# The upper right block of the second weight kept whole, with smaller output and score buffers, six attention visits moved, and the last product cut into column pieces

## The chip, the cores and the metric

The kernel runs on one core of a Trainium2 chip. The metric is the device time of one execution in microseconds (us). A core has five engines that run side by side: TensorE (PE in the profile; PEld are its weight loads), VectorE (DVE), ScalarE (ACT), GpSimd (POOL) and the sync engine (SP), beside the DMA engines that move data. Matrix products land in PSUM banks and are brought from there into SBUF by DVE or ACT.

## The reference

```python
scores = scale * np.matmul(q, k.transpose(0, 1, 3, 2))      # 8 batches, 12 heads, 448 x 448
attn = np.maximum(scores, 0.0) ** 2 / S
x = np.matmul(attn, v)                                      # back to [8, 448, 768]
...
xn = (x - mu) / np.sqrt(var + 1e-06) * g_ln                 # per row of 768
ch = np.maximum(xn @ w_ch1, 0.0) @ w_ch2                    # 768 -> 3072 -> 768
return x + ch
```

## The kernel before

**Work and tiles.** The work is done in bf16 with sums in fp32. A batch b has 6 pairs of heads. The pairs are taken in two halves, so that a batch has three attention steps, numbered n = 3b to 3b + 2 over all batches, and each step has seven key blocks s. `att_QK(n, s)` makes one score tile with four 64-row products (L587). One activation on ACT (L596) or DVE (L598) scales it and applies the relu, and takes it from one of three PSUM slots into a score buffer in SBUF. A square in place follows (L611 on DVE, L613 on POOL). `att_AV(n, s)` multiplies the squared tile with v: 28 products for the seven s of a step (L649). A copy (L363 or L365) takes the result out.

**The feed forward part.** `ffn_1` multiplies the normalised batch with w1, 24 column blocks of six products (L930). Each block's relu is written to `h1` by ACT (L946) or DVE (L948), over two PSUM banks in turn, so that a block waits for the relu of the one before the last. The second product, of 24 row chunks of w2, is made in tiles of 128 rows and in two column halves of 384. For batches 0 and 1, and for one tile m = 2 of each later pair of batches, `ffn_2` does it plainly with 24 products a half (L1200), and DVE takes each half out with the row scale and the residual (L1217). For the other tiles of batches 2 to 7 `ffn_w` takes two tiles together by the scheme of seven products for eight: named P1, P2, P6, P5, P7, P3 and P4, with 12 matmuls of 384 columns each (L1122), two PSUM banks named x and y, and evacuations on DVE named c1, C11, c2, p5, C22, C12 and C21 (L1136). It needs differences of the four blocks of w2 (`b11`, `b12` upper left and right, `b21`, `b22` below), named T1 to T4 and made once by `make_sums` (L988, on DVE or POOL), and differences of the rows of `h1` (L1082, the S operations on DVE).

**T1 and the five extra products.** T1 is b12 - b11, in 12 chunks. Seven chunks have a home in a staging buffer. The last five are written over b12 itself. From then on the upper right block of w2 is no longer whole, so the second column half of a plain tile of batches 2 to 7 takes b12 as T1 + b11: five more products of the same rows of `h1` with `b11`, that is 29 matmuls where the first half has 24.

**Buffers.** Score tiles come from a pool of `N_AT` = 9 buffers of 128x896 bf16. Output tiles come from a pool of two of 128x768 fp32, with one of 128x384 (`o_half`) beside it. `store_tile` writes each with two DMAs of 64 rows (L1239), on ACT's queue. The last tile alone has one of its two on SP's.

**Who sets the order.** The instruction order of each engine is written out ahead by a planner in the kernel (`Order`) with a cost for each operation, and each engine then runs its list in order. `segment` mixes the steps of the feed forward part of batch b with the attention of batch b + 1. The attention is cut into visits, and a visit is due when the feed forward work done has reached its share (`due`). The visit that matters here, one for each step n from 7 on except those that begin a batch without a predecessor in progress, is

```python
        if prev:
            return head + [qks(n, 0, 2) + av_of(n - 1) + qks(n, 2, 4), qks(n, 4, 7)]
```

that is on PE: 8 matmuls of L587 for (n, 0) and (n, 1), the 28 of L649 for step n - 1, then 8 of L587 for (n, 2) and (n, 3). With three PSUM slots, (n, 2) waits for the relu of (n, 0), and (n, 3) for the relu of (n, 1). There are 16 such visits with the score buffers of batches 2 to 7: n = 7, 8, 10, 11 and 12 to 23.

Of the kernel before, what the change touches and what calls it, by code (L numbers as in the profile page):

```python
# [199 lines left out]
def kernel(  # L200
# [10 lines left out]
    nc = tc.nc  # L211
# [22 lines left out]
    FIRST_ORDER = "qqaqaqqqqqqaaaqaqaaqaqaqqqaaaqaaqaaqqaaqqaaaaaaaa"  # L234
    N_O = 2
    SUMMED = [0] + [2] + [NPER] * (B - 2)
# [6 lines left out]
    v_pool = ctx.enter_context(tc.tile_pool(name="v", bufs=1))  # L243
    at_pool = ctx.enter_context(tc.tile_pool(name="attn", bufs=N_AT))
    xc_pool = ctx.enter_context(tc.tile_pool(name="xc", bufs=1))
    s_pool = ctx.enter_context(tc.tile_pool(name="small", bufs=4))
    o_half = ctx.enter_context(tc.tile_pool(name="oh", bufs=1))
    o_pool = ctx.enter_context(tc.tile_pool(name="o", bufs=N_O))
    ps_s = ctx.enter_context(tc.tile_pool(name="ps_s", bufs=3, space=bass.MemoryType.PSUM))
# [5 lines left out]
    g_sb = const_pool.tile([P, K1], fp32)  # L255
    g_rows = const_pool.tile([K1, P], fp32)
    ident_f = const_pool.tile([K1, K1], fp32)
    w1 = w_pool.tile([P, K1, d_ff], bf16)
    w2 = w_pool.tile([P, K2, d_model], bf16)
    h1 = w_pool.tile([P, K2, S + T], bf16)  # L260
    sum_t = const_pool.tile([P, S], fp32)
    rsum_t = const_pool.tile([P, S], bf16)
    xT_all = const_pool.tile([P, J * d_model], bf16)
    x_all = const_pool.tile([P, J, d_model], bf16)
# [215 lines left out]
    attn = {}  # L480
    at_ring = [None] * N_AT
    held = []
    held_relu = []

    def wait_for_x(ev):
# [4 lines left out]
        else:  # L490
            held_relu.append(ev)

    def at_use(last):
        at_ring.pop(0)
        at_ring.append(last)

# [72 lines left out]
    def att_QK(n, s):  # L569
# [4 lines left out]
        def emit(eng):  # L574
            if b == 1 and s >= J - 3:
                if (n, s) == (NPER, J - 3):
                    attn["more"] = big(STAGE[0], None, i=6, r=2, c=S)
                attn[n, s] = attn["more"][:, 3 * (pn % 2) + s - (J - 3)]
            else:
                a = at_pool.tile([P, 2, S], bf16, tag="attn")  # L580
                attn[n, s] = a
            sc = ps_s.tile([P, 2, 512], fp32, tag="s")
            st[0] = sc
            for r in range(2):
                qT = qkT[b][rows_of(r), 0].rearrange("p (j t) c -> p j t c", t=NPER)
                for half in range(2):
                    nc.tensor.matmul(  # L587
                        sc[rows_of(half), r, :S],
                        qkT[b][rows_of(r), 1, s * NPER + pn, rows_of(half)],
                        qT[:, :, pn, rows_of(half)], start=True, stop=True)  # L590

        op = R.pe(195.0, emit, qk_dep(n, s) + [slots[0], at_ring[0]], "Q")

# [27 lines left out]
        slot_use(ev)  # L621
        at_use(None)
        if early:
# [332 lines left out]
    o_st = {}  # L956
    o_ring = [DONE] * N_O

# [24 lines left out]
    def make_sums():  # L983
# [49 lines left out]
        for k, o, d in pieces(t4):  # L1033
            for i in range(o.shape[1]):
                made["T4", k + i] = run(o[:, i:i + 1], b21[:, k + i:k + i + 1],
                                        tw["T2", k + i].rearrange("p (o c) -> p o c", o=1), True, [made["T2", k + i]] + d, 5.2)
        for k in range(J):
            tw["T1", k] = stage["cols"][:, 1, k]
        for a, z in ((0, 3), (3, 5), (5, J)):
            made["T1", a] = run(stage["cols"][:, 1, a:z], b12[:, a:z], b11[:, a:z], True,  # L1040
                                w2_ld + [later("turn", 3, 1)], 5.3)
        for k, n in ((J, 3), (J + 3, 2)):
            for i in range(k, k + n):
                tw["T1", i] = b12[:, i]
            made["T1", k] = run(b12[:, k:k + n], b12[:, k:k + n], b11[:, k:k + n], True,
                                done3 + [later("f2_end", 0)], 5.3)
        for name in ("T1", "T2", "T3", "T4"):
# [47 lines left out]
    def ffn_w(u, m, name, part):  # L1095
# [8 lines left out]
        if name == "P1" and part == 0:  # L1104
            if when(f_banks[0]) > when(f_banks[1]):
                f_banks.reverse()
                f_tags.reverse()
            e["y0"] = f_banks[1]
        bank = "x" if name in ("P1", "P6", "P7", "P4") else "y"
        w = {"P1": lambda k: b11[:, k], "P2": lambda k: b21[:, k], "P6": lambda k: tw["T2", k], "P5": lambda k: tw["T1", k],  # L1110
# [16 lines left out]
        def evac(key, tile_n, cols, r, more, deps):  # L1127
            def emit(eng):
                if key == "c1":
                    o_t = o_pool.tile([P, d_model], fp32, tag="o")  # L1130
                    e["o", 0] = o_t
                elif key == "p5":
                    o_t = o_half.tile([P, hd], fp32, tag="oh")
                    e["o", 1] = o_t
                o = e["o", 1] if key in ("p5", "C22") else e["o", 0][:, cols]
                nc.vector.scalar_tensor_tensor(o, e["ps", bank], r, o if more else xm[u, m + tile_n][:, cols],  # L1136
                                               op0=Alu.mult, op1=Alu.add)
            e[key] = R.add("DVE", 620.0, emit, [op, ops["rstd", b]] + deps, key=-3.0)
            return e[key]

        if name == "P1":
            e["S1"] = [s_op(u, m, "S1", x, [op, e["S2"][x]]) for x in range(2)]
            evac("c1", 0, lo, r1, False, [o_ring[-N_O]])
        elif name == "P2":
            e["S4"] = [s_op(u, m, "S4", x, [op, e["S2"][x]]) for x in range(2)]
            ev = evac("C11", 0, lo, r1, True, [e["c1"]])
            e["C11 out"] = store_tile(u, m, lo, ev, False, lambda: e["o", 0][:, lo])
        elif name == "P6":
            evac("c2", 0, hi, r1, False, [e["c1"]])
            s2_last = [op, e["S1"], e["S4"]]  # L1150
# [6 lines left out]
        elif name == "P5":  # L1157
            evac("p5", 1, hi, r2, False, [half_free[0]])
        elif name == "P7":
            ev = evac("C22", 1, hi, r2, True, [e["p5"]])  # L1160
            half_free[0] = store_tile(u, m + 1, hi, ev, False, lambda: e["o", 1])
        elif name == "P3":
            ev = evac("C12", 0, hi, r1, True, [e["c2"], e["C11"]])
            e["C12 out"] = store_tile(u, m, hi, ev, False, lambda: e["o", 0][:, hi])
        else:
            ev = evac("C21", 1, lo, r2, False, [e["C11 out"]])
            f_banks[:] = [e["C12"], ev]
            f_tags.reverse()
            o_ring.append([e["C12 out"], store_tile(u, m + 1, lo, ev, final, lambda: e["o", 0][:, lo])])
            if m == 3:  # L1170
# [4 lines left out]

    def part_of(u, j, part, parts):
        n = K2 if u == 0 or j == 0 else K2 + KH - J
        return slice(part * n // parts, (part + 1) * n // parts)

    def f2_deps(u, m, j, part, parts):  # L1180
        b = 2 * u + (0 if m < 3 else 1)
        z = min(part_of(u, j, part, parts).stop, K2) - 1
        d = [ops["w2", z], ops["h", b, z]]
# [4 lines left out]
    def ffn_2(u, m, j, part, parts):  # L1188

        b = 2 * u + (0 if m < 3 else 1)  # L1190
        ks = [(k, w2[:, k, j * hd:(j + 1) * hd]) for k in range(K2)]
        if u > 0 and j == 1:
            ks = [(k, b11[:, k]) for k in range(J, KH)] + ks

        def emit(eng):
            if part == 0:
                o_ps = f_tile([P, hd], fp32)
                o_st["ps"] = o_ps
            for i, (ki, w) in list(enumerate(ks))[part_of(u, j, part, parts)]:
                nc.tensor.matmul(o_st["ps"], stat(u, m, ki), w, start=(i == 0), stop=(i == len(ks) - 1))  # L1200
        run = part_of(u, j, part, parts)
        op = R.pe(162.5 * (run.stop - run.start), emit, f2_deps(u, m, j, part, parts) + (ops["sums", "T1"] if u > 0 and j == 1 else []))
        if m in (2, 6) and j == 1 and part == parts - 1:
# [6 lines left out]
        ri = m if m < 3 else m - 3  # L1210

        def evac(eng):
            if j == 0:
                o_t = o_pool.tile([P, d_model], fp32, tag="o")
                o_st[u, m] = o_t
            cols = slice(j * hd, (j + 1) * hd)
            nc.vector.scalar_tensor_tensor(o_st[u, m][:, cols], ps, rstd[b][:, ri:ri + 1], xm[u, m][:, cols],  # L1217
                                           op0=Alu.mult, op1=Alu.add)
        ev = R.add("DVE", 620.0, evac, [op, ops["rstd", b], o_ring[-N_O]], key=-3.0)
        f_use(ev)  # L1220
        if j == 1:
            if m in (2, 6):
                now_known(ev, "f2_out", b)
            if m == 3:
                ops["m3_out", u] = ev
            o_ring.append(store_tile(u, m, slice(0, d_model), ev, False, lambda: o_st[u, m]))

    half_free = [DONE]

    def store_tile(u, m, cols, ev, final, src):  # L1230
# [5 lines left out]
        for r, (bb, jj) in enumerate(blocks):  # L1236
            def store(eng, r=r, bb=bb, jj=jj):
                dst = out[2 * u + bb].rearrange("(p j) d -> j p d", j=J)[jj, :, cols]
                (nc.scalar if eng == "ACT" else nc.sync).dma_start(dst, src()[rows_of(r)])  # L1239
            sto = R.add("SP" if final and r else "ACT", 550.0, store, [ev], key=-0.5, load=(T, 150.0))  # L1240
# [69 lines left out]
    def f2_steps(u, ms):  # L1310
        return [("f2", u, m, j, p, n) for m in ms for j in range(2)
                for n in [PARTS if u == 0 or j == 0 else 5] for p in range(n)]

# [3 lines left out]
    def segment(steps, visits, then, margin, ahead=True, hooks=()):  # L1317
# [5 lines left out]
        while i < len(steps) or done < n_v or not centered:  # L1323
# [7 lines left out]
            if done == n_v and not centered:  # L1331
                tC = start_of(mean_deps(then) + [slots[0]])
                if tC <= now + 60.0:
                    center(then)
                    centered = True
                    continue
            due = done < n_v and prog >= (total - margin) * done / n_v
            if min(tF, tV, tC) >= FAR:
# [171 lines left out]
```

## Time and profile before

| | |
|---|---|
| median of 3 runs | 530.66 us (530.31 to 530.81) |
| the profiled execution | 530.49 us, of which the span is 528.6 us |
| PE busy | 513.4 us, 97% of the span |
| DVE, ACT, POOL busy | 341.5, 227.0 and 117.3 us |
| granted TensorE clock | 0.998 of full speed |
| DMA | 51.91 MB read, 11.01 MB written |

The profile is of one execution. Its span goes from the first to the last instruction, and 1.9 us of its time lie around it. "Busy" is the time in which an engine has an instruction under way. Ends of matmuls are modelled, so that neighbouring ones overlap: how long one takes in a stream is read from the starts.

### The profile page before, as it was taken

What the parts mean: (1) busy time and instruction counts of PE and PEld (TensorE: products, weight loads), DVE (VectorE), ACT (ScalarE), POOL (GpSimd) and SP (SyncE); (2) the same over time, 40 slices, a digit from 0 to 9 for tenths busy, and PEclk for the clock granted to TensorE, in tenths of its full rate; (3) what the DMA queues carried; (4) which work ended last, traced back from release to release, by engine and by line L of the source; (5) the groups of instructions that cost most, each with busy time, mean ns of one, the idle gap of its engine ahead of it and who ended that gap; (6) DMA issues with size and microseconds to landing.
All of it is one profiled execution on the core that took longest, in us unless ns stands there. A gap on an engine that the chain in (4) does not pass through costs nothing.

```text
span 528.6 us, 9882 instructions
## 1 busy us (share of the span) xinstructions
PE 513.4 (97%) x4107; PEld 276.9 (52%) x4107; DVE 341.5 (65%) x632; ACT 227.0 (43%) x361; POOL 117.3 (22%) x132
## 2 busy tenths in 40 slices
PE   5899999999999999999999999999999999999996
PEld 3444455555564455545555455644556445555553
DVE  5988647438996667773877666666578646534352
ACT  5978611124314653275323663156531655124300
POOL 7411600401342222230250320403210202100000
PEclk9999999999999999999999999999999999999999
DMA  9999999988198902979079920989024400241022
GB/s 193 197 188 199 199 191 165 171 101 135 34 164 126 105 2 43 157 117 97 16 111 127 122 54 16 164 128 104 4 38 99 82 1 0 61 73 19 1 62 60
DMA packets 144121, 51.83 MB, mean 98 GB/s; under 512 B 121798, under 2 KB 142028, under 8 KB 144076
## 3 DMA queue, kind: packets, MB, share of 16 engines
q0 software_dynamic: 81072, 25.50, 45.4%
q1 hardware_dynamic: 55724, 14.79, 17.6%
q10 hardware_dynamic: 7280, 10.92, 8.4%
q8 instruction: 32, 0.52, 0.4%
q14 instruction: 13, 0.11, 0.1%
HBM read 51.91 MB, written 11.01 MB: 119 GB/s over the span
## 4 chain that ended last, share of the span: by engine, by line
PE 93%; DVE 4%; ACT 1%; DMA 1%; issue 0%; ACTq 0%; DVEq 0%
PE f_ps L930 40%; PE f_ps L1122 23%; PE f_ps L1200 15%; PE sc L587 6%; PE ps L649 5%; DVE a L611 2%; ACT a L596 1%; DVE t L365 1%; DMA f<-in_q_dram 1%; PE ps L508 1%; PE f_ps L910 0%; PE ps L711 0%; DVE st L792 0%; DVE st L791 0%; PE f_ps L508 0%
## 5 line engine op out<-in xcount | busy, mean ns | idle before, releaser
L930 PE MATMUL f_ps<-a,w 128*128 128x448 bf16 x1134 | 220.7, 353 | 0.6 <-DVE h L948 0.6
L930 PEld LDWEIGHTS <-w 128*128 128x128 bf16 x1134 | 108.3, 98 | 108.6 <-issue 11.0
L596 ACT ACTIVATE a<-sc 128x896 bf16<-128x896 f32 x117 | 103.4, 927 | 81.9 <-PE sc L587 75.9
L946 ACT ACTIVATE h<-f_ps 128x448 bf16<-128x448 f32 (+1 forms) x156 | 83.2, 534 | 106.5 <-PE f_ps L930 105.2
L611 DVE TENSOR_TENSOR a<-a 128x896 bf16<-128x896 bf16 x156 | 100.6, 683 | 1.4 <-ACT a L596 1.4
L1122 PEld LDWEIGHTS <-h 128*128 128x128 bf16 x648 | 62.8, 98 | 43.8 <-issue 2.4
L598 DVE TENSOR_SCALAR a<-sc 128x896 bf16<-128x896 f32 x42 | 45.6, 1087 | 41.2 <-PE sc L587 41.1
L1122 PE MATMUL f_ps<-w,h 128*128 128x384 bf16 x369 | 65.2, 326 | 0.0
L1200 PE MATMUL f_ps<-w,h 128*128 128x384 bf16 x351 | 58.7, 326 | 0.0
L587 PE MATMUL sc<-t 64*64 64x448 bf16 x672 | 49.0, 365 | 4.0 <-ACT a L596 2.4
L1200 PEld LDWEIGHTS <-h 128*128 128x128 bf16 x351 | 33.9, 98 | 23.8 <-issue 1.7
L740 POOL TENSOR_TENSOR sum_t<-sum_t,xT_all 128x384 f32<-128x384 f32 (+2 forms) x25 | 20.0, 799 | 94.6 <-ACT xT_all L363 94.6
L1136 DVE SCALAR_TENSOR_TENSOR o_t<-f_ps,r_t,x_all 128x384 f32<-128x384 f32 x36 | 22.1, 614 | 18.6 <-PE f_ps L1122 18.3
L587 PEld LDWEIGHTS <-t 64*64 64x64 bf16 x672 | 17.7, 106 | 28.3 <-issue 21.8
L401 POOL DMA_DIRECT2D t<-in_k_dram x12 | 20.0, 1901 | 52.7 <-DMA t<-t 52.7
L649 PE MATMUL ps<-a,v_t 64*64 64x448 bf16 x552 | 29.8, 350 | 0.0
L1217 DVE SCALAR_TENSOR_TENSOR o_t<-f_ps,r_t,x_all 128x384 f32<-128x384 f32 x20 | 12.3, 613 | 26.4 <-PE f_ps L1200 26.3
L363 ACT CAST xT_all<-ps 128x768 bf16<-128x768 f32 (+2 forms) x34 | 20.7, 614 | 19.9 <-PE ps L649 18.1
L649 PEld LDWEIGHTS <-v_t 64*64 64x64 bf16 x672 | 19.7, 107 | 13.5 <-issue 2.8
L401 POOL DMA_DIRECT2D t<-in_q_dram x12 | 19.3, 1774 | 31.4 <-DMA t<-t 30.1
L1136 DVE SCALAR_TENSOR_TENSOR o_t<-f_ps,r_t,o_t 128x384 f32<-128x384 f32 x27 | 16.6, 614 | 14.8 <-PE f_ps L1122 14.7
L848 ACT ACTIVATE a<-a,g_sb 128x448 bf16<-128x448 bf16 x19 | 11.6, 659 | 30.3 <-DVE a L841 15.1
(91 smaller groups left out, 411.8 us busy)
## 6 DMA issues: line engine op xcount, KB each, us to landing
out_dram<-o_t ACTq DMA_DIRECT2D x71, 96.0 KB, 2.2
v_t<-in_v_dram POOLq DMA_DIRECT2D x16, 336.0 KB, 6.1
w<-in_moe_w_ch_dram POOLq DMA_DIRECT2D x4, 1152.0 KB, 39.0
t<-in_q_dram POOLq DMA_DIRECT2D x12, 336.0 KB, 8.6
t<-in_k_dram POOLq DMA_DIRECT2D x12, 336.0 KB, 6.8
out_dram<-o_t ACTq DMA_DIRECT2D x20, 192.0 KB, 5.5
w<-in_moe_w_ch_dram POOLq DMA_DIRECT2D x4, 768.0 KB, 19.3
w<-in_moe_w_ch_dram POOLq DMA_DIRECT2D x1, 1536.0 KB, 28.9
```

The costliest lines, as they stand in the source:

```text
L363: nc.scalar.copy(o, i)
L401: nc.gpsimd.dma_start(stage["cols"][half * T:(half + 1) * T, t if b < 4 else 0].rearrange("p j (h d) -> p j h d", d=D), src[b, half * 6:ha ...
L587: nc.tensor.matmul(sc[rows_of(half), r, :S], qkT[b][rows_of(r), 1, s * NPER + pn, rows_of(half)], qT[:, :, pn, rows_of(half)], start=True, ...
L596: nc.scalar.activation(attn[n, s], st[0][:, :, :S], Act.Relu, scale=rc2)
L598: nc.vector.tensor_scalar(attn[n, s], st[0][:, :, :S], rc2, 0.0, op0=Alu.mult, op1=Alu.max)
L611: nc.vector.tensor_mul(attn[n, s], attn[n, s], attn[n, s])
L649: nc.tensor.matmul(av_st[n][half][rows_of(hh)], vt[b][rows_of(half), 2 * pn + hh, s * D:(s + 1) * D], attn[n, s][rows_of(half), hh, :], st ...
L930: nc.tensor.matmul(st[0], w1[:, ki, ni * P:(ni + 1) * P], xc[b][:, ki, :], start=(i == 0), stop=(i == K1 - 1))
L946: nc.scalar.activation(o, st[0][:, c], Act.Relu)
L1122: nc.tensor.matmul(e["ps", bank], a(k), w(k), start=new and k == 0, stop=k == KH - 1, skip_group_check=True)
L1136: nc.vector.scalar_tensor_tensor(o, e["ps", bank], r, o if more else xm[u, m + tile_n][:, cols], op0=Alu.mult, op1=Alu.add)
L1200: nc.tensor.matmul(o_st["ps"], stat(u, m, ki), w, start=(i == 0), stop=(i == len(ks) - 1))
```

## The change

- The last five chunks of T1 get a home of their own, at the end of one large buffer (`at_all`) that also holds the score tiles. So b12 stays whole, and `ffn_2` uses 24 products in both column halves, in all batches.
- The score tiles are slices of `at_all` in turn: nine while b < 2, and eight for b >= 2, since the ninth lies where the home of T1's last chunks is.
- Outputs use two tiles of 128x768 (`o_all`) and no half tile: the pair of `ffn_w` writes both, its second tile's right half into the other one, and each half of each tile is waited for by itself (`o_done`). `g_rows` becomes a slice of `sum_t`.
- `HELD` shifts the point at which six visits are due, by -2 to +4 in units of 1000 ns of planned feed forward work. Its keys are (n, 0) for n = 13, 15, 16, 19, 21 and 22.
- The very last P4 is made in two column pieces by `last_product`: 256 columns into bank x as before, then 128 columns into bank y from zero. What bank x holds for those 128 columns is taken out ahead (`early`). Each piece has its own evacuation and two stores, one on ACT's queue and one on SP's.

```diff
+    HELD = {(13, 0): -2, (15, 0): -1, (16, 0): 3, (19, 0): 4, (21, 0): -1, (22, 0): 3}
...
-    at_pool = ctx.enter_context(tc.tile_pool(name="attn", bufs=N_AT))
-    o_half = ctx.enter_context(tc.tile_pool(name="oh", bufs=1))
-    o_pool = ctx.enter_context(tc.tile_pool(name="o", bufs=N_O))
...
+    g_rows = sum_t[:K1, :P]
+    at_all = const_pool.tile([P, (N_AT - 1) * 2 * S + 5 * (d_model // 2)], bf16)
+    o_all = const_pool.tile([P, 2, d_model], fp32)
...
-                a = at_pool.tile([P, 2, S], bf16, tag="attn")
-                attn[n, s] = a
+                i = at_next[0] % (N_AT if b < 2 else N_AT - 1)
+                at_next[0] = i + 1
+                attn[n, s] = at_all[:, i * 2 * S:(i + 1) * 2 * S].rearrange("p (r c) -> p r c", r=2)
...
-        for k, n in ((J, 3), (J + 3, 2)):
-            for i in range(k, k + n):
-                tw["T1", i] = b12[:, i]
-            made["T1", k] = run(b12[:, k:k + n], b12[:, k:k + n], b11[:, k:k + n], True,
-                                done3 + [later("f2_end", 0)], 5.3)
+        at_end = at_all[:, (N_AT - 1) * 2 * S:].rearrange("p (k c) -> p k c", c=hd)
+        for a, z in ((0, 3), (3, 5), (5, J), (J, 10), (10, KH)):
+            o = stage["cols"][:, 1, a:z] if a < J else at_end[:, a - J:z - J]
+            for k in range(a, z):
+                tw["T1", k] = o[:, k - a]
+            made["T1", a] = run(o, b12[:, a:z], b11[:, a:z], True, w2_ld + [later("turn", 3, 1), later("av_done", 1)], 5.3)
...
+            e["turn"] = o_take()
+            e["o", 0], e["o", 1] = o_all[:, e["turn"]], o_all[:, 1 - e["turn"]]
...
+    def last_product(u, m, part, e, r2, deps):
+        c = (slice(0, 2 * P), slice(2 * P, hd))[part]
+        o = e["o", 0][:, c]
+        if part == 0:
+            def early(eng):
+                c1 = slice(2 * P, hd)
+                nc.vector.scalar_tensor_tensor(e["o", 0][:, c1], e["ps", "x"][:, c1], r2, xm[u, m + 1][:, c1],
+                                               op0=Alu.mult, op1=Alu.add)
+            e["early"] = R.add("DVE", 310.0, early, [e["P7 end"], e["C11 out"]], key=-3.0)
+        ps = e["ps", "x"][:, c] if part == 0 else e["ps", "y"][:, :P]
+        def emit(eng):
+            for k in range(KH):
+                nc.tensor.matmul(ps, stat(u, m + 1, KH + k), tw["T4", k][:, c], start=part == 1 and k == 0, stop=k == KH - 1,
+                                 skip_group_check=True)
+        op = R.pe(KH * (110.0, 57.0)[part], emit, deps + ([e["early"]] if part == 0 else [e["C12"]]))
+        def evac(eng):
+            nc.vector.scalar_tensor_tensor(o, ps, r2, xm[u, m + 1][:, c] if part == 0 else o, op0=Alu.mult, op1=Alu.add)
+        ev = R.add("DVE", (470.0, 310.0)[part], evac, [op, e["C11 out"]], key=-3.0)
+        store_tile(u, m + 1, c, ev, True, e["o", 0])
...
-        ks = [(k, w2[:, k, j * hd:(j + 1) * hd]) for k in range(K2)]
-        if u > 0 and j == 1:
-            ks = [(k, b11[:, k]) for k in range(J, KH)] + ks
...
+            for ki in range(part * K2 // parts, (part + 1) * K2 // parts):
+                nc.tensor.matmul(o_st["ps"], stat(u, m, ki), w2[:, ki, j * hd:(j + 1) * hd],
+                                 start=(ki == 0), stop=(ki == K2 - 1))
...
-            due = done < n_v and prog >= (total - margin) * done / n_v
+            due = done < n_v and prog >= (total - margin) * done / n_v + 1000.0 * HELD.get(visits[done][0][1:3], 0)
```

## The prediction

> **What bounds the kernel now.** I read the busy rows first, then the table of busy time by stage, the chain that ended last, and the timeline of the stages that the change touches. From the page and from the chain:
>
> ```profile
> PE 513.4 (97%) x4107; PEld 276.9 (52%) x4107; DVE 341.5 (65%) x632; ACT 227.0 (43%) x361; POOL 117.3 (22%) x132
> PE 93%; DVE 4%; ACT 1%; DMA 1%; issue 0%; ACTq 0%; DVEq 0%
> ...
> L1200 PE MATMUL f_ps<-w,h 128*128 128x384 bf16 x351 | 58.7, 326 | 0.0
> ...
> 96.30 17.55 PE f_ps L1200 x108
> ```
>
> PE is busy 97% of the span and makes 93% of the chain. So a matmul removed after the first 33 us is time saved, and a stall of PE is time lost. One matmul of L1200 takes 326 ns, but they overlap: 108 of them follow each other in 17.55 us, or 162.5 ns each. The table by stage (us, then busy us and count of each engine) shows where PE is not full:
>
> ```profile
> 195.50:221.20 25.70, 25.70 (x199) 14.78 (x200) 19.40 (x34) 7.76 (x13) 9.71 (x12) 1.00 0.78 93
> 221.20:255.00 33.80, 33.51 (x257) 16.91 (x250) 21.40 (x37) 21.91 (x37) 9.16 (x8) 1.00 0.74 91
> ...
> 345.40:380.00 34.60, 33.76 (x257) 16.94 (x258) 22.16 (x38) 22.23 (x37) 7.54 (x7) 1.00 0.73 89
> ```
>
> The lost time lies in some visits. First a visit that flows (n = 10), then one that stalls (n = 13); columns are start, length, engine and line:
>
> ```profile
> 179.12 1.49 PE L649 MATMUL ps<-a,v_t 64*64 64x448 bf16 x28
> 179.34 1.09 DVE L598 TENSOR_SCALAR a<-sc 128x896 bf16<-128x896 f32 x1 [1.65 <-PE sc L587]
> 180.44 0.55 PE L587 MATMUL sc<-t 64*64 64x448 bf16 x8
> ...
> 230.40 1.72 ACT L596 ACTIVATE a<-sc 128x896 bf16<-128x896 f32 x2
> 231.52 0.36 PE L587 MATMUL sc<-t 64*64 64x448 bf16 x4
> 232.17 0.38 PE L587 MATMUL sc<-t 64*64 64x448 bf16 x4 [0.29 <-ACT a L596]
> ```
>
> In the first, the relu of (n, 1) runs on DVE beside the 28 products, and the next eight score products start together. In the second DVE was in its statistics (L791), both relus ran one after the other on ACT, and the last four products start 0.65 us after the four before them. When nothing holds them the distance is 0.19 us, so 0.46 us is lost. The bracket shows only 0.29 since matmul ends are modelled. By starts, the same happens for n = 16 (295.80, 0.45), 19 (356.38, 0.39) and 22 (420.77, 0.45). For n = 15 and 21 ACT was issuing two stores when the relu of (n, 0) came, and the score products start 1.52 us after L649 (266.92 to 268.44, 391.89 to 393.41) in place of 1.32: 0.19 each. After n = 19 comes one more:
>
> ```profile
> 358.12 5.24 DVE L611 TENSOR_TENSOR a<-a 128x896 bf16<-128x896 bf16 x6
> 363.28 0.61 DVE L948 TENSOR_SCALAR h<-f_ps 128x448 bf16<-128x448 f32 x1
> 363.94 0.92 PE L930 MATMUL f_ps<-a,w 128*128 128x448 bf16 x4 [0.60 <-DVE h L948]
> ```
>
> Six squares stand on DVE ahead of the relu that PE's next block needs; by starts 0.76 us are lost. Together: 0.46 + 0.45 + 0.39 + 0.45 + 0.19 + 0.19 + 0.76 = 2.89 us, all at the six visits that `HELD` names. The end:
>
> ```profile
> 522.03 0.81 PE L1122 MATMUL f_ps<-c_t,h 128*128 128x384 bf16 x4
> ...
> 524.18 0.62 DVE L1136 SCALAR_TENSOR_TENSOR o_t<-f_ps,r_t,x_all 128x384 f32<-128x384 f32 x1 [1.33 <-PE f_ps L1122]
> 524.83 0.55 SPq L1239 DMA_DIRECT2D out_dram<-o_t  x1
> ```
>
> The last P4 starts at 522.03, its evacuation ends at 524.80, its stores follow, and the span ends at 528.6.
>
> **What the Trainium skill says.** "TensorE: Matmul & The Clock Gate", section "Back-to-back issue gap", gives N/2.4 + 2.5 ns from one matmul to the next: 162.5 ns at N = 384, which the trace shows. It also gives some 81 ns sustained at N = 128, where the weight load counts; no matmul of 128 columns with a full weight is in this trace. Its section "Architectural detail: the array is 16× 32×32, not 1× 128×128" says that ScalarE and VectorE run strictly first in, first out. The trace agrees: the relu at 363.28 sat behind squares. "DMA: Bandwidth & Descriptors", section "Latency and other measured facts", puts the fixed cost of a DMA at about 2 us; the 96 KB stores here land a median 2.2 us after issue, so a smaller store saves little.
>
> **The change part by part.**
>
> *The extra products go.* Three tiles (m = 2 of three pairs of batches) lose five each: 15 x 162.5 ns = 2.44 us, all on PE's path, as PE doesn't idle in these stretches (the 195.50 row is full). Value -2.44.
>
> *The six visits.* I compared the built order of each engine around each visit. In all 16 visits the relu of (n, 1) now stands on DVE. For 13, the visit comes ahead of the statistics; for 16, 19 and 22 behind them. In 15 and 21 the relu of (n, 0) stands ahead of the stores. The block behind n = 19 has its relu on ACT. Is DVE free in time? For n = 16, the statistics started at 292.75, 6.2 us after the stage's L930 began at 286.57, held by a DMA. Three tiles of 1.2 us and one S of 0.55 end at 10.4. The visit begins after 54 matmuls of 188.5 ns, at 10.2, and its relu can't start before 11.0: 0.6 spare. For n = 19 the last statistics ended 12.1 us after its L930 began at 346.08, and the visit comes after 66 matmuls, at 12.4. The two pairs of stores (1.12 us a pair) lie beside the 28 products. So all of it can go: between -2.9 and -1.4 (half); value -2.9.
>
> *Eight score buffers.* This adds a wait. The buffer of (n, 1) is now that of (n - 1, 0), which `att_AV` still reads in the same visit. In the built program all 16 DVE relus of such visits wait for the fourth of the 28 products; before, they waited for their own scores alone. For n = 10 in the trace: the fourth product ends at 179.48 (modelled), the own scores at 179.29, and DVE started 0.05 after that. New start 179.53, end 180.62, release of PE at 180.67, where its natural time is 180.63: 0.04 us. Behind the waiting relu stand squares whose reader comes a visit later; who waits for it is PE's (n, 3). The other ten visits with a DVE relu give 0.03 to 0.05. Cost 16 x 0.04 = +0.64; the ends are 0.3 (0.02 each) and 1.6 (0.1 each).
>
> *Sums.* The last two pieces of T1 now run on DVE before the centering of batch 2 (0.75 + 0.61 = 1.36 us, the rows of L988 for these sizes), where before one of 0.75 ran later on DVE and one of 1.64 on POOL. The subtractions and gains then end at some 158.3, not 156.9; the first product of batch 2 starts at 161.57. 0, hidden by 3 us of L1200; without that cover at most 1.4. Two squares of 1.68 move from POOL to DVE at 0.53 to 0.6: hidden.
>
> *Outputs.* Each half of an output tile is rewritten five products (9.7 us) or more after the store that frees it, and a store takes 0.55 to issue and 2.2 to land: 0. The same DMAs go out on ACT's queue; SP's gets one more, at the end. `g_rows` in `sum_t` is read at 26 us and overwritten much later: 0.
>
> *The last product.* 12 matmuls of 256 columns at 109 ns take 1.31 us, 12 of 128 at 56 to 98 ns (98 is the length of one weight load, if none overlapped) 0.7 to 1.2 us; I take 81, 0.97, so PE ends 0.33 later than with 1.95. The evacuation of 128 columns is an estimate from its row: 614 ns less 256 columns at 1.04 ns is 0.35, in place of 0.62. It ends 0.06 later, but the first piece's stores are long out, and the last one has 32 KB for 96 KB. The `early` copy runs under P3. Between -0.7 and +0.3; value -0.2.
>
> *Small waits* at moved places that the rows don't show: 0 to 0.6, value +0.2 (an evacuation on ACT that ends just when PE's next block needs its bank, as after n = 13).
>
> Sum: -2.44 - 2.9 + 0.64 - 0.2 + 0.2 = -4.7. Against the profiled execution's 530.49: 525.8. It lies 0.17 below the median of the runs, so the new median may be 525.8 to 526.0. I give **525.8**.
>
> **Rivals.** *The stalls only move.* DVE is busy 65% and ACT 43%; a visit moved by some us can meet other evacuations or stores. Then `HELD` brings nothing: -2.44 + 0.64 - 0.2 + 0.2 = -1.8, 528.7. For it: planned times put the stalls into the program in the first place. Against it: the order and the room above. Chance 0.14.
>
> *Slower: the wait for the score buffer decides.* If the DVE relu started only when all 28 products are through (179.12 + 1.49 = 180.61, not 179.48), it would end 1.13 later, and PE would lose 1.17 at each of 16 visits: +18.7, or 544 in all. It decides from a loss of 0.33 a visit on (5.3 / 16). Against it: the wait is on the fourth product, and its end is seen in the trace only as a modelled one. Chance 0.05.
>
> *No net change*: half of the stalls stay and a visit costs 0.2 us through relus late on DVE: -2.44 - 1.4 + 3.2 = -0.6, about 529.9. Chance 0.03.
>
> **How the numbers follow.** Main case 0.78: 524.9 to 527.2 by the ends above. Stalls moved 0.14, 527 to 529. A range of **524.8 to 527.9** holds the main case and the nearer half of that rival, and leaves out about 0.15. A measurement here tells 0.2%, 1.1 us, from no change: faster than 529.6 has 0.91, between 529.6 and 531.7 0.03, slower 0.06.
>
> **What would show it.** L1200's successor with 15 matmuls fewer; no idle of PE in the stages 221 to 255, 286 to 320, 345 to 380 and 411 to 445, other than some 0.04 by starts at each visit; the DVE relu of (n, 1) starting 0.2 later after its scores; the last evacuation at about 0.35 us. A gap over 0.2 us between the two groups of four score products in most visits would make it wrong, and so would new waits of L930 on a relu behind the moved visits.

## The result and the profile after

The changed kernel takes 525.46 us (median of five runs, 525.42 to 526.57), beside 530.66 us before (530.27 to 531.58). The ratio is 0.9905, with an interval of 0.989 to 0.9919: faster by 5.2 us or 1%. The forecast was 525.8 us. Of the two profiled executions the spans are 528.58 and 523.68 us, 4.90 us apart.

From the page of the profile after, the busy row, the chain by engine, and the rows of L595 and L1212 (L598 and L1200 before):

```profile
PE 511.1 (98%) x4104; PEld 277.2 (53%) x4104; DVE 348.7 (67%) x647; ACT 220.4 (42%) x350; POOL 116.3 (22%) x130
...
PE 95%; DVE 2%; ACT 1%; DMA 1%; issue 0%; ACTq 0%; DVEq 0%
...
L595 DVE TENSOR_SCALAR at_all<-sc 128x896 bf16<-128x896 f32 x50 | 54.4, 1088 | 42.1 <-PE ps L645 22.8
L1212 PE MATMUL f_ps<-w,h 128*128 128x384 bf16 x336 | 56.3, 326 | 0.0
```

The plain second product has 336 matmuls for 351: fifteen are gone. Eight relus went from ACT to DVE (50 of L595 for 42), and DVE now waits for PE at a new place, `ps` of L645: these are the products with v. In the table by stage (us, then busy us and count of PE, PEld, DVE, ACT and POOL, granted clock, DMA share and GB/s) PE is full where it was not:

```profile
195.50:221.20 25.70, 25.70 (x203) 14.67 (x201) 20.21 (x34) 6.89 (x11) 9.04 (x11) 1.00 0.78 93
221.20:254.20 33.00, 33.00 (x249) 16.86 (x246) 21.10 (x39) 20.99 (x36) 7.64 (x7) 1.00 0.82 93
343.90:377.90 34.00, 34.00 (x256) 17.45 (x253) 22.80 (x41) 20.91 (x36) 8.04 (x8) 1.00 0.80 91
```

In the list of PE's waits after 33 us stood five before, 1.7 us together; in the changed kernel that list, which holds waits over 0.15 us, is empty. This is the visit of n = 13 in the timeline after (start, length, engine, line, operation):

```profile
227.06 0.57 PE L584 MATMUL sc<-t 64*64 64x448 bf16 x8
...
227.47 1.49 PE L645 MATMUL ps<-at_all,v_t 64*64 64x448 bf16 x28
227.67 0.91 ACT L593 ACTIVATE at_all<-sc 128x896 bf16<-128x896 f32 x1
227.88 1.09 DVE L595 TENSOR_SCALAR at_all<-sc 128x896 bf16<-128x896 f32 x1 [3.43 <-PE ps L645]
...
228.79 0.62 PE L584 MATMUL sc<-t 64*64 64x448 bf16 x8
...
229.34 0.55 PE L926 MATMUL f_ps<-a,w 128*128 128x448 bf16 x2
```

The relus of (n, 0) and (n, 1) lie beside each other on ACT and DVE, and all eight last score products stand in one entry. By starts the second four come 0.23 us after the first four (at 229.03, for 228.79), not the 0.65 of before, but not the free 0.19 either. All sixteen visits show this 0.23. And the end of the program:

```profile
517.60 0.60 PE L1187 MATMUL f_ps<-c_t,h 128*128 128x256 bf16 x4
...
518.91 0.39 PE L1187 MATMUL f_ps<-c_t,h 128*128 128x128 bf16 x4
519.11 0.48 DVE L1192 SCALAR_TENSOR_TENSOR o_all<-f_ps,r_t,x_all 128x256 f32<-128x256 f32 x1 [0.69 <-PE f_ps L1187]
519.13 0.50 PE L1187 MATMUL f_ps<-xT_all,h 128*128 128x128 bf16 x6
519.47 0.28 PE L1187 MATMUL f_ps<-x_all,h 128*128 128x128 bf16 x2
519.62 1.19 SPq L1250 DMA_DIRECT2D out_dram<-o_all  x2
519.78 0.35 DVE L1192 SCALAR_TENSOR_TENSOR o_all<-f_ps,r_t,o_all 128x128 f32<-128x128 f32 x1 [0.19 <-PE f_ps L1187]
```

From the start of the last product to the end of the span it was 6.55 us before (528.58 - 522.03); it is 6.08 now (523.68 - 517.60). The last evacuation ends 2.53 us after that start, for 2.77 before: that is 0.24 of the 0.47 us, and the other 0.23 lie behind it, where the last stores carry 32 KB each for 96.

### The profile page after: what moved, and what is told of

It is laid out like the page before. It is cut to its first block, busy times and chain, and to the rows that moved or that the text cites. A ratio compares the mean times of both kernels' runs of the same rounds, so it can differ in the third digit from the quotient of the medians.

```text
span 523.7 us, 9887 instructions
## 1 busy us (share of the span) xinstructions
PE 511.1 (98%) x4104; PEld 277.2 (53%) x4104; DVE 348.7 (67%) x647; ACT 220.4 (42%) x350; POOL 116.3 (22%) x130
## 4 chain that ended last, share of the span: by engine, by line
PE 95%; DVE 2%; ACT 1%; DMA 1%; issue 0%; ACTq 0%; DVEq 0%
PE f_ps L926 42%; PE f_ps L1122 23%; PE f_ps L1212 15%; PE sc L584 7%; PE ps L645 5%; DVE at_all L608 1%; DVE t L365 1%; DMA f<-in_q_dram 1%; ACT at_all L593 1%; PE ps L504 1%; PE f_ps L906 0%; PE f_ps L1187 0%; PE ps L707 0%; PE f_ps L504 0%; PE slot L816 0%
## 5 line engine op out<-in xcount | busy, mean ns | idle before, releaser
L926 PE MATMUL f_ps<-a,w 128*128 128x448 bf16 x1134 | 220.6, 353 | 0.0
L926 PEld LDWEIGHTS <-w 128*128 128x128 bf16 x1134 | 108.3, 98 | 107.1 <-issue 9.4
L593 ACT ACTIVATE at_all<-sc 128x896 bf16<-128x896 f32 x109 | 95.9, 922 | 78.7 <-PE sc L584 71.6
L608 DVE TENSOR_TENSOR at_all<-at_all 128x896 bf16<-128x896 bf16 x158 | 99.6, 666 | 2.0 <-ACT at_all L593 1.8
L1122 PEld LDWEIGHTS <-h 128*128 128x128 bf16 x636 | 61.6, 98 | 42.6 <-issue 2.2
L595 DVE TENSOR_SCALAR at_all<-sc 128x896 bf16<-128x896 f32 x50 | 54.4, 1088 | 42.1 <-PE ps L645 22.8
L1212 PE MATMUL f_ps<-w,h 128*128 128x384 bf16 x336 | 56.3, 326 | 0.0
L1122 PE MATMUL f_ps<-w,h 128*128 128x384 bf16 x324 | 56.1, 326 | 0.0
L1212 PEld LDWEIGHTS <-h 128*128 128x128 bf16 x336 | 32.5, 98 | 22.6 <-issue 1.5
L736 POOL TENSOR_TENSOR sum_t<-sum_t,xT_all 128x384 f32<-128x384 f32 (+2 forms) x25 | 21.6, 863 | 85.9 <-ACT xT_all L363 85.9
L1130 DVE SCALAR_TENSOR_TENSOR o_all<-f_ps,r_t,x_all 128x384 f32<-128x384 f32 x35 | 21.5, 615 | 16.8 <-PE f_ps L1122 16.5
L734 POOL TENSOR_TENSOR sum_t<-xT_all 128x384 f32<-128x384 bf16 (+2 forms) x13 | 11.8, 984 | 84.5 <-ACT xT_all L363 84.4
L645 PE MATMUL ps<-at_all,v_t 64*64 64x448 bf16 x552 | 29.8, 350 | 0.0
L1230 DVE SCALAR_TENSOR_TENSOR o_all<-f_ps,r_t,x_all 128x384 f32<-128x384 f32 x20 | 12.3, 613 | 24.6 <-PE f_ps L1212 24.6
L645 PEld LDWEIGHTS <-v_t 64*64 64x64 bf16 x672 | 19.8, 107 | 13.5 <-issue 2.8
L1130 DVE SCALAR_TENSOR_TENSOR o_all<-f_ps,r_t,o_all 128x384 f32<-128x384 f32 x27 | 16.6, 615 | 13.7 <-PE f_ps L1122 13.6
```

What stands on the lines that cost most here:

```text
L593: nc.scalar.activation(attn[n, s], st[0][:, :, :S], Act.Relu, scale=rc2)
L595: nc.vector.tensor_scalar(attn[n, s], st[0][:, :, :S], rc2, 0.0, op0=Alu.mult, op1=Alu.max)
L608: nc.vector.tensor_mul(attn[n, s], attn[n, s], attn[n, s])
L645: nc.tensor.matmul(av_st[n][half][rows_of(hh)], vt[b][rows_of(half), 2 * pn + hh, s * D:(s + 1) * D], attn[n, s][rows_of(half), hh, :], st ...
L736: nc.gpsimd.tensor_add(s0, s0, x0)
L926: nc.tensor.matmul(st[0], w1[:, ki, ni * P:(ni + 1) * P], xc[b][:, ki, :], start=(i == 0), stop=(i == K1 - 1))
```

## The measure used for the experiments

Times of one kernel can differ by one or two us between executions, and part of that comes from the first 33 us. There PE runs the same 433 matmuls in all these kernels, yet the first F1 block (L926, L930 before) begins at 32.9 or 33.0 us in nine of the thirteen profiles and at 33.4 to 34.0 in four. So beside the median I give the **stretch**, from the start of that first block to the start of the last product, and the **tail** from there to the end of the span. What PE loses "by starts" is the distance between the starts of two matmuls less what it is where nothing waits. Each ratio is to the runs of the kernel before that were timed in the same round, whose medians lie between 530.66 and 530.75 us.

| kernel | median us (all runs) | ratio to before, interval | stretch | tail |
|---|---|---|---|---|
| before | 530.66 (530.27 to 531.58) | | 489.09 | 6.55 |
| changed | 525.46 (525.42 to 526.57) | 0.9905 (0.989 to 0.9919) | 484.67 | 6.08 |
| nine_shared | 524.93 (524.39 to 525.79) | 0.9889 (0.9876 to 0.9903) | 483.57 | 6.1 |
| seven | 529.36 (529.23 to 530.06) | 0.9971 (0.996 to 0.9982) | 488.44 | 6.1 |
| swap | 525.91 (525.02 to 526.24) | 0.9904 (0.989 to 0.9918) | 484.09 | 6.1 |
| swap_all | 526.51 (526.02 to 527.7) | 0.9923 (0.991 to 0.9936) | 485.35 | 6.1 |
| swap_most | 524.84 (524.67 to 525.41) | 0.9891 (0.9879 to 0.9904) | 483.84 | 6.1 |
| no_held | 530.02 (529.38 to 531.74) | 0.999 (0.998 to 0.9999) | 488.92 | 6.1 |
| held19 | 527.29 (527.13 to 527.4) | 0.9935 (0.9923 to 0.9947) | 486.34 | 6.1 |
| held_only | 528.44 (528.03 to 528.56) | 0.9953 (0.9941 to 0.9966) | 486.78 | 6.55 |
| in_place_nine | 527.08 (526.77 to 529.02) | 0.9941 (0.9926 to 0.9957) | 486.58 | 6.1 |
| whole_last | 527.38 (525.91 to 527.53) | 0.9931 (0.9917 to 0.9945) | 484.64 | 6.57 |
| split64 | 525.71 (525.68 to 525.73) | 0.9904 (0.989 to 0.9918) | 484.64 | 6.32 |

## What eight score buffers cost

**One buffer more, one fewer.** nine_shared changes the count and finds room by overlaying chunks of T1; seven takes one buffer away.

```diff
-                i = at_next[0] % (N_AT if b < 2 else N_AT - 1)
+                i = at_next[0] % (N_AT if b < 2 else N_AT - 2)       # seven
+                i = at_next[0] % (N_AT)                              # nine_shared, with
...
+    at_all = const_pool.tile([P, N_AT * 2 * S + 3 * (d_model // 2)], bf16)
...
+        at_end = at_all[:, N_AT * 2 * S:].rearrange("p (k c) -> p k c", c=hd)
...
+            o = stage["cols"][:, 1, a:z] if a < J else at_end[:, a - J - 2 * (a == 10):z - J - 2 * (a == 10)]
```

> The changed kernel with nine score buffers in all batches. For this the last two chunks of T1 are written to the place of the two chunks before them, so that the products that read chunks 8 to 11 of T1 read two chunks' worth of data in place of four: this part of the result is changed, and no instruction is left out. Theory (the price of eight buffers is the wait of the DVE relu of (n, 1) for the fourth product with v): the relus wait for their own scores alone again, and 0.64 us (the prediction's sum) to 0.85 us (the gaps between the starts of score products in the changed kernel) come off: 524.6 to 524.8 us. Rival (the wait is hidden, the gaps have another cause): 525.4 us.

> The changed kernel with seven score buffers for b >= 2 in place of eight. In the built order the DVE relu of (n, 1) now waits for the eighth product with v in each visit, and the ACT relu of (n, 0) for the fourth. Theory (the time of this wait is handed to PE as soon as the relu ends after PE's own time): four products more are 0.21 us later, at each of 16 visits: 525.5 + 3.4 = 528.9 us, with a distance of some 0.4 us between the two groups of four score products where the changed kernel has 0.22. Rival (waits of this size lie beside other work): under 0.3 us in all, 525.7 us.

With nine the stretch is 1.10 us shorter, with seven 3.77 us longer. The visit of n = 13 with nine, then with seven:

```profile
226.73 0.57 PE L584 MATMUL sc<-t 64*64 64x448 bf16 x8
...
227.35 1.09 DVE L595 TENSOR_SCALAR at_all<-sc 128x896 bf16<-128x896 f32 x1 [3.24 <-PE sc L584]
...
228.93 0.74 PE L926 MATMUL f_ps<-a,w 128*128 128x448 bf16 x3
```

```profile
228.47 0.57 PE L584 MATMUL sc<-t 64*64 64x448 bf16 x8
...
229.47 1.09 DVE L595 TENSOR_SCALAR at_all<-sc 128x896 bf16<-128x896 f32 x1 [3.62 <-PE ps L645]
...
230.93 0.55 PE L926 MATMUL f_ps<-a,w 128*128 128x448 bf16 x2
```

The bracket names what DVE waited for: its own scores with nine buffers (`sc`), the products with v with fewer (`ps`). From the first score product to the next F1 block the visit takes 2.21 us with nine, 2.28 with eight (227.06 to 229.34) and 2.46 with seven, and all sixteen visits of a kernel agree within 0.01 us. Over sixteen visits 0.067 us each makes 1.07 of the 1.10 us. For seven, 0.19 each beyond eight is 3.02. The rest is two waits of L926 for a relu on DVE, which were not in the theory. The list of seven's waits after 33 us has this one row (total, times, longest):

```profile
PE f_ps L926 <- DVE h L944: 0.5, 2, 0.2
```

By starts these two, at 316.55 and 440.74, cost 0.39 us each, so that the sum is 3.80 for the 3.77 measured. Both rivals (a wait of this size is hidden) fall. But the first step is hidden in part: DVE's relu starts 0.62, 0.81 and 1.00 us after the first score product with nine, eight and seven buffers. Its first 0.19 us of delay costs PE 0.07 a visit, the second 0.19 costs the whole 0.19.

**The same wait on a faster engine.** If the price is the end of the waiting relu, it should vanish when that relu is 0.17 us shorter. ACT takes 0.91 us where DVE takes 1.09, so I gave (n, 0) to DVE and (n, 1) to ACT, still with eight buffers.

```diff
-        late = FAR if n == 0 and s < K_NEAR else 0.0 if s == 1 and n >= 2 * NPER else 600.0
+        late = FAR if n == 0 and s < K_NEAR else -400.0 if s == 0 and n > 2 * NPER and n != 3 * NPER else 600.0   # swap
...
+        engs = ("DVE",) if lead and s == 0 else ("ACT",) if lead and s == 1 else ("ACT", "DVE")   # swap_all
...
+        late = FAR if n == 0 and s < K_NEAR else -400.0 if s == 0 and n in SWAPPED else 0.0 if s == 1 and n >= 2 * NPER and n not in SWAPPED else 600.0   # swap_most
```

`late` is what the planner adds to DVE's finish when it chooses between ACT and DVE. In swap_all `lead` holds for the sixteen visits and leaves no choice; in swap_most SWAPPED is 7, 8, 10 to 14, 16, 17, 19, 20, 22 and 23, so that n = 15, 18 and 21 keep the old preference.

> The changed kernel with another preference between the engines: the relu of (n, 0) is to stand on DVE and that of (n, 1) on ACT in the visits that end a step (in the built order 13 of the 16 visits take it, three keep DVE for (n, 1)). The relu that waits for the fourth product with v is then the one of ACT, 0.91 us for 1.09, and DVE's begins with its own scores. Theory (the price of eight buffers is the end of the waiting relu on DVE, 0.053 to 0.068 us after PE's own time): 0.1 us earlier is enough to take it off PE's path, 13 visits x 0.053 to 0.068 = 0.7 to 0.9 us less: 524.6 to 524.8 us, and the two groups of four score products 0.19 us apart in these visits. Rival (the order around the visits shifts and new stalls of PE eat it): 525.5 us or more.

> As the last one, but with no choice: (n, 0) on DVE and (n, 1) on ACT in all 16 visits, however late the engine is. Theory (the waiting relu alone counts): 16 visits x 0.053 to 0.068 = 0.85 to 1.1 us less, 524.4 to 524.6 us. Rival (where DVE or ACT is late, having no choice costs more than the wait did): some visits show 0.2 to 0.5 us of idle PE, and the total is 525 us or more.

> The changed kernel with the relus swapped, (n, 0) on DVE and (n, 1) on ACT, in twelve or thirteen visits, and the old preference kept for n = 15, 18 and 21. Theory (the run with the preference for all gained 0.58 us from the first L926 to the last product, with 0.29 us given back at n = 18, where both relus had gone to ACT): 0.8 us less than the changed kernel from the first L926 to the last product, 524.7 us where the first 33 us are alike. Rival (the gain is within what the orders differ by): 525.2 to 526 us.

By its time swap is no gain. Its trace shows why: the stretch is 0.58 us shorter, but its first F1 block began at 34.03, 1.1 us late, and at n = 18 both relus went to ACT, with 0.30 us of PE lost. Its times then fit the rival, its trace the theory. swap_all is the miss. Other operations moved, and in the tile before batch 2 an output (L1233) stood on DVE behind pieces of the centering (L840):

```profile
155.79 2.69 DVE L840 TENSOR_TENSOR a<-xT_all,sum_t 128x768 bf16<-128x768 bf16 x3
158.40 0.61 DVE L1233 SCALAR_TENSOR_TENSOR o_all<-f_ps,r_t,x_all 128x384 f32<-128x384 f32 x1
...
159.06 0.65 PE L1215 MATMUL f_ps<-w,h 128*128 128x384 bf16 x3 [0.81 <-DVE o_all L1233]
```

By starts PE lost 0.98 us there, and 0.30 us at 154.19. Having no choice did cost more than the wait, as its rival said, but only one visit is a place that the rival named: at n = 19 DVE was in its statistics, and the visit takes 0.22 us over the free 2.21. swap_most has neither fault; its visit of n = 13 (its lines stand one further down):

```profile
226.81 0.57 PE L585 MATMUL sc<-t 64*64 64x448 bf16 x8
...
227.24 1.09 DVE L596 TENSOR_SCALAR at_all<-sc 128x896 bf16<-128x896 f32 x1 [3.05 <-PE sc L585]
227.62 0.92 ACT L594 ACTIVATE at_all<-sc 128x896 bf16<-128x896 f32 x1
...
229.01 0.93 PE L927 MATMUL f_ps<-a,w 128*128 128x448 bf16 x4
```

The visit takes 2.21 us again, as with nine buffers. ACT's relu ends at 228.54, not the 228.97 - 0.25 = 228.72 that DVE's would have (the changed kernel's, moved to this visit's start). Twelve of the sixteen visits take 2.21 us; the four that kept DVE for (n, 1), n = 7, 15, 18 and 21, still take 2.28. Twelve times 0.067 is 0.80 us, and the stretch is 0.83 us shorter than that of the changed kernel. So the end of the waiting relu is the cause. The median is 0.6 us below that of the changed kernel, but the intervals of the two ratios overlap: the trace shows this gain, the times alone do not.

## What the shifted visits bring

**HELD taken away, and put back for one visit.**

```diff
-    HELD = {(13, 0): -2, (15, 0): -1, (16, 0): 3, (19, 0): 4, (21, 0): -1, (22, 0): 3}
+    HELD = {}                       # no_held
+    HELD = {(19, 0): 4}             # held19
```

> The changed kernel with HELD empty: every visit is due where it was before; all the rest of the change stays. Theory (the six shifts end the stalls): in the built order four of the sixteen relus of (n, 1) stand on ACT again, and the stalls after n = 13, 15, 16, 19, 21 and 22 come back, 2.9 us or a little less, since with five products fewer in each of three tiles the visits do not stand quite where they stood before: about 528.2 us, with PE idle again in the stages of these visits. Rival (the stalls only moved, HELD brings nothing): 525.5 us, as the changed kernel.

> The changed kernel with HELD cut to its one entry for n = 19. In the built order the relu of (n, 1) of n = 19 is on DVE again, and three relus of the block of squares stand between the statistics and the differences of h where six squares in a row stood without HELD. Theory (each entry acts on its own stage alone; without any of them the stage of n = 19 loses 2.1 us): 2.1 us of the 4.25 us that came back without HELD are gone again: 525.5 + 2.1 = 527.6 us, no idle PE over 0.1 us in the stage of n = 19, and the stalls of n = 13, 16 and 22 as they were without HELD. Rival (shifting one visit moves the stall to another block of the stage or to the next stage): 528.5 us or more.

Without HELD the stretch grows by 4.25 us, not 2.9. The rival "HELD brings nothing" falls. By starts the gaps at n = 13, 15, 16, 21 and 22 are the 0.46, 0.19, 0.46, 0.19 and 0.46 us that the kernel before had. At n = 19 it is more: 0.40 between the score products, and then

```profile
363.65 0.54 ACT L942 ACTIVATE h<-f_ps 128x448 bf16<-128x448 f32 x1 [0.79 <-PE f_ps L926]
364.52 0.61 DVE L944 TENSOR_SCALAR h<-f_ps 128x448 bf16<-128x448 f32 x1
365.05 0.61 DVE L608 TENSOR_TENSOR at_all<-at_all 128x896 bf16<-128x896 bf16 x1
365.18 1.10 PE L926 MATMUL f_ps<-a,w 128*128 128x448 bf16 x5 [1.63 <-DVE h L944]
```

The relu of h at 364.52 stood behind squares that DVE had worked at since 359.43; by starts PE lost 1.79 us, where the kernel before lost 0.76 in the same way. Another 0.44 us of the 4.25 is not HELD's: at 166.29 us PE waited for ACT, which had taken 2.34 us over the issue of two stores, against 1.90 in held19, whose order is the same there. So HELD is worth about 3.8 us in this kernel.

held19 confirms it. With its one entry the gaps of n = 19 are gone, those of 13, 16 and 22 (0.46 each) and of 15 and 21 (0.19) stay, and the stretch is 2.58 us shorter than without HELD: 2.15 for n = 19 (0.36 in the visit and 1.79 behind it), and the 0.44. Nothing moved elsewhere, against the rival.

**HELD alone, and the extra products brought back.** held_only adds to the kernel before just the line of HELD and its term in `due`. in_place_nine takes the changed kernel and brings back T1 over b12, the five extra products of each of three tiles, and nine buffers:

```diff
+            due = done < n_v and prog >= (total - margin) * done / n_v + 1000.0 * HELD.get(visits[done][0][1:3], 0)   # held_only
...
-    at_all = const_pool.tile([P, (N_AT - 1) * 2 * S + 5 * (d_model // 2)], bf16)                                      # in_place_nine
+    at_all = const_pool.tile([P, N_AT * 2 * S], bf16)
...
-        at_end = at_all[:, (N_AT - 1) * 2 * S:].rearrange("p (k c) -> p k c", c=hd)
...
+        for k, n in ((J, 3), (J + 3, 2)):
+            for i in range(k, k + n):
+                tw["T1", i] = b12[:, i]
...
+        if u > 0 and j == 1:
+            ks = [(k, b11[:, k]) for k in range(J, KH)] + ks
```

> The kernel before with the table HELD and its shift of the due point alone: nine score buffers from the pool, T1 over b12 with its fifteen extra products, and the last product whole. Theory (the shifts alone end the stalls and need nothing else of the change): 530.7 - 2.9 = 527.8 us. Rival (the shifts fit only the order that the other edits make, and new stalls take the place of the old ones): between 529.5 and 530.7 us.

> The changed kernel with T1 again in place over b12, the fifteen extra products and nine score buffers in all batches; HELD, the output halves and the last product in pieces stay. Theory (each edit has its own price): fifteen products cost 15 x 162.5 ns = 2.44 us, and the wait for a score buffer, 1.09 us in the trace without it, goes: 1.35 us more than the changed kernel between the first L926 and the last product, about 526.8 us. Rival (HELD fits only the order with 24 products, as the run of HELD on the kernel before suggests): the stall of 0.76 us after n = 13 is there as well, 2.1 us more, 527.5 us.

held_only gains 2.31 us of stretch; its theory had 2.9. All six visits flow, and the gap behind n = 19 is gone. But soon after the visit of n = 13 PE loses 0.76 us, at a place where the kernel before lost nothing. The timeline of held_only there:

```profile
231.47 0.80 ACT L364 CAST xT_all<-ps 128x768 bf16<-128x768 f32 x1 [0.90 <-DMA x_all<-xT_all]
...
232.16 0.55 ACT L947 ACTIVATE h<-f_ps 128x448 bf16<-128x448 f32 x1
...
232.76 1.30 PE L931 MATMUL f_ps<-a,w 128*128 128x448 bf16 x6 [0.59 <-ACT h L947]
```

A copy into `xT_all` stood first on ACT and waited for the transposing DMA that still read that tile; behind it stood the relu that PE needed. In the changed kernel one relu of h stands ahead of that copy, and the DMA landed 8.5 us after its issue, not 9.6. in_place_nine shows the same gap at the same place (232.55, 0.57 us over a free step; DMA 9.4 us), and its stretch is longer than that of nine_shared by 3.01 us: 15 x 162.5 ns = 2.44 for the products, 0.57 for this wait. So the price of the products is confirmed. The shift of n = 13 by -2 leaves a wait in both orders with 29 products in a half and none in the changed kernel's: the rivals of both runs hold in part. Whether the later landing or the order on ACT is the deeper cause was not separated.

## The last product

whole_last takes the last P4 in one piece again; split64 cuts it at column 320.

```diff
-        if final and name == "P4":                                   # whole_last
-            last_product(u, m, part, e, r2, deps)
-            return
...
-        c = (slice(0, 2 * P), slice(2 * P, hd))[part]
+        c = (slice(0, hd - 64), slice(hd - 64, hd))[part]            # split64
```

> The changed kernel with the last P4 whole, as before: twelve products of 384 columns into bank x, one evacuation, two stores. All the rest of the change stays. Theory (column pieces shorten the way from the start of the last product to the end of the span by 0.47 us, as the two traces show: 6.57 before, 6.10 after): 525.5 + 0.5 = 525.9 us. Rival, the prediction's own size of this step: 525.7 us. Rival (the stores that follow set the end, so pieces bring nothing): 525.5 us.

> The changed kernel with the last P4 cut at column 320 in place of 256: pieces of 320 and 64 columns. Theory (these products cost their columns alone, a new weight each time costs nothing more): 64 columns follow each other every 29 ns, PE ends when it did, and the last evacuation takes some 0.28 us for 0.35: 0.05 to 0.1 us less, 525.4 us, hardly to be told by the times, but plain in the trace. Rival (under 128 columns the load of a new weight sets the rate, at 56 ns or more): the last twelve products take 0.67 us or more for 0.35, and the end comes 0.25 us or more later: 525.7 us or more.

In the trace of whole_last the tail is 6.57 us, for 6.55 before, and its stretch is that of the changed kernel: the pieces are worth 0.47 to 0.49 us. Its times fell in two groups, 525.9 to 526.0 and 527.4 to 527.5; the profile is of the first, which fits. What makes the second group 1.5 us longer is open, since no trace is of it; the median of 527.4 is not evidence on the last product. split64's tail is 6.32, 0.24 more than the changed kernel's:

```profile
519.23 0.28 PE L1187 MATMUL f_ps<-c_t,h 128*128 128x64 bf16 x4
519.35 0.34 PE L1187 MATMUL f_ps<-xT_all,h 128*128 128x64 bf16 x6
519.43 0.55 DVE L1192 SCALAR_TENSOR_TENSOR o_all<-f_ps,r_t,x_all 128x320 f32<-128x320 f32 x1 [1.01 <-PE f_ps L1187]
...
519.90 0.27 DVE L1192 SCALAR_TENSOR_TENSOR o_all<-f_ps,r_t,o_all 128x64 f32<-128x64 f32 x1
520.01 1.42 SPq L1250 DMA_DIRECT2D out_dram<-o_all  x2
```

Four matmuls of 64 columns begin within 0.12 us (519.23 to 519.35), 29 ns each, with a new weight for each: the rival that a weight load sets the rate falls. Still the theory missed. The first evacuation, now of 320 columns, ends at 519.98, for 519.59 in the changed kernel. It keeps DVE from the last one, which ends at 520.17, for 520.13, and SP's two stores begin 0.39 us later, at 520.01, and take 1.42 us to issue for 1.19. Of the two cuts tried, that at 256 keeps the first piece from holding up the second.

## Why the prediction was right, step by step

**The extra products** (-2.44): right. From the last F1 product of batch 2 to the first of batch 3 the time went from 26.54 us (195.20 to 221.74) to 25.79 (195.50 to 221.29); five products are 0.81 and one visit's wait gives 0.07 back. in_place_nine agrees.

**The six visits** (-2.9): right in place, and 0.2 us too small. All the listed gaps are gone. From the first score product to the block behind, the six visits took 2.33 us more than the free 2.21 each, and the gap behind n = 19 was 0.77: 3.10 in all. The list of 2.89 left out that the block behind also comes 0.024 us later in each of the six, 0.15 together; the other 0.06 is in the rounding of the starts. What the step did not say is that those gaps belong to one order: with the rest of the change but no HELD they are worth 3.8 us, and HELD on the kernel before opens a wait of 0.76 us at n = 13. The rival "the stalls only move" is wrong for this kernel, but for held_only it is right at that visit.

**Eight score buffers** (+0.64): right mechanism, too small. The relu did start 0.19 us later than before, as forecast. What I priced, the start of the second four score products, comes 0.04 us later a visit, as forecast too. The term failed in what it left out: the block behind comes later by another 0.024 us (0.316 for 0.292 us after those products). That is 0.067 a visit, 1.07 in all, where nine_shared measures 1.10. The bounds, 0.3 and 1.6, held it. The same 0.024 shows behind the six stalled visits of before, so it is a fixed cost of score products that start late, whether by 0.04 or by 0.46 us. The slower rival, a wait for all 28 products, did not occur; seven shows that a longer wait is passed on, at 0.19 us more a visit, under that rival's 0.33.

**The last product** (-0.2): 0.47 measured. The mis-sized term is the one matmul of 128 columns, taken as 81 ns. Ten of them begin within 0.56 us (518.91 to 519.47), 56 ns each, the lower bound of the step. The second piece so takes 0.67 us for 0.97, and that 0.30 covers the 0.27 by which the forecast was off. The Trainium skill gives both numbers in "TensorE: Matmul & The Clock Gate", section "Back-to-back issue gap": its formula N/2.4 + 2.5 ns, there for a matmul without its weight load, gives 56, and for a stream with weight loads it gives 81. The trace has such a stream, of twelve matmuls with a weight load each, and the formula holds in it. The estimate of the last evacuation, 0.35 us, is what the row shows.

**Small waits** (+0.2): none over 0.05 us appeared. Sums and outputs at nothing: no wait of PE for them appeared.

The sum by these measurements is -2.44 - 3.10 + 1.07 - 0.47 = -4.94, for a span that went from 528.58 to 523.68, 4.90 less; the 0.04 between them is one F1 block that came 0.04 us late, at 165.08. Each step had the mechanism right, but for the pace of the 128-column products. That the total of -4.7 came so near is partly luck: the buffers cost 0.43 us more than forecast, and the visits, the last product and the small waits gave 0.20, 0.27 and 0.20 more.

## What to carry to other kernels

When PE is full, count the time from the first product of a visit to the first product after it, not one distance within it: a relu that ended 0.19 us later came through as 0.04 us at the score products and 0.02 more at the block behind. Where the order is planned ahead, a hand shift belongs to the order that it was found in, so try it again after each other edit. And if a waiting operation can run on two engines, give it the one that does it in less time and give the other to its neighbour that doesn't wait, but only where both are free: here ACT takes 0.91 us for that relu and DVE 1.09.

## What the runs showed of the hardware

Matmuls with a 128 x 128 weight, new each time, follow each other every 29 ns at 64 columns (twelve in split64), 56 at 128 (twelve in the changed kernel) and 162.5 at 384 (108 in the kernel before), though the record of one weight load is 98 ns long: loads overlap, and down to 64 columns the loads do not set the pace in these streams. Two stores of one tile took between 1.90 and 2.34 us to issue on ACT's queue at the same place in two executions, which was enough to stop PE for 0.44 us once. And the first 33 us of one and the same list of PE instructions took between 32.9 and 34.0 us. In swap, products with v at 14.2 us (and the score products between them) followed each other at half the usual rate for nearly 2 us, four in 0.37 us for 0.19. The clock record of its trace grants the full clock from 16.0 us on, where the usual rate begins; in the other traces that is between 10.0 and 13.7 us. The other three late starts had waits: seven waited 0.8 us for the load of v, and no_held and swap_all 0.7 and 0.8 us more than the changed kernel for a copy on DVE.
